# A delta-rule attention with a GELU block behind it: three narrow groups per slot in program order

## The chip, the cores and the metric

The kernel runs on one core of a Trainium2 chip. The metric is the device time of one execution in microseconds. Before the change it is 835.21 us, the median of three runs (832.89 to 837.22). The profiled execution spans 828.9 us; all times inside it count from its first instruction. Engines are TensorE (PE in the profile, its weight loads PEld), VectorE (DVE), ScalarE (ACT), GpSimd (POOL) and SyncE (SP, which issues most transfers).

## What is computed

```python
# attention: B, H, S, D = 4, 8, 768, 48
k_n = k / (norm(k, axis=-1) + 1e-6)
for t in range(S):
    y[:, :, t] = q[:, :, t] @ state                       # 48 x 48 state per batch and head
    v_old      = state^T @ k_n[:, :, t]
    state      = state + beta[:, :, t] * outer(k_n[:, :, t], v[:, :, t] - v_old)
# block: x is y as (3072, 384); w_in 384 x 2048, w_out 2048 x 384
h = x @ w_in
out = (h / (1 + exp(-1.702 * h))) @ w_out
```

The kernel does the recurrence in chunks of 128 positions: 6 chunks of 4 batches are 24 *units*. Inside a chunk it needs the scores of keys against keys (G), the inverse of a triangular 128 x 128 matrix per head (in four 32 x 32 diagonal blocks, which VectorE inverts for two units at a time, and a forward substitution over the four blocks on TensorE), and the masked scores of queries against keys (M). Two consecutive units together give 256 rows for the block behind.

## The kernel before

Work on TensorE is *wide* (the two big products, full 128 x 128 array, `ph` and `po`) or *narrow* (attention, on parts of the array). The program is a loop of slots, n from -1 to 24. In slot n three units are under way: A = n-1 (last substitution, outputs, new state), B_ = n (middle of its substitution), D_ = n+1 (scores, first block). Wide work waits in `queue`, a list of generators that yield the estimated cost of what they have just issued.

```python
class Engine:                       # an operation is pinned to the program's order if in_order[0]
    def __getattr__(self, name):
        op = getattr(self.engine, name)
        return pinned(op) if in_order[0] else op
vec, act, pe = Engine(nc.vector), Engine(nc.scalar), Engine(nc.tensor)
```

An operation that is not pinned is placed by the scheduler of the build, which may move it ahead of earlier ones that it takes to be waiting. Before, only slots up to 1 are pinned (`in_order[0] = n < HB`, HB = 2).

```python
def slot(n, share):                                        # GR = 6 groups
    A, B_, D_ = steps.pop(n - 1, None), steps.get(n), None
    P = prepare(n + B) if B <= n + B < len(units) else iter(())     # B = 4
    ...
    for group in range(GR):
        if group == 0:
            next(P, None)                                  # transposes of the keys
            D_ = steps.get(n + 1) or new_step(n + 1)
            next(D_.scored, None)                          # transposes of the queries
        elif group == 1:
            together([(B_, 1)], [(A, 2)])
            next(D_.scored, None)                          # first half of psQ
        elif group == 2:
            run(D_.scored)                                 # second half of psQ
        elif group == 3:
            together([(A, 3), (D_, 0)], [(B_, 1)])
            run(P)                                         # psG
        elif group == 4:
            if A: A.queries(); A.outputs()                 # psY
        else:
            together([(B_, 2)], [(D_, 0)])
            if A: A.state()                                # psS
        ...                                                # normalizing of later keys, from group 2
        if group == GR - 1 and n % HB == 1:
            m = n + 1 + HB
            if B <= m < len(units):
                inverting = invert(*units[m], HB)
        ahead_of(inverting, 5 if n % HB == 1 else 4)       # so many steps of the inversion
        ...                                                # conversion of weights, slots up to 3
        for cost in take(todo / (GR - group)):             # wide work
            todo -= cost
    if n % HB == 0:
        run(inverting)
    ...                                                    # loads; new wide work goes to the queue
```

The narrow operations, with the lines that the profile names:

```python
def together(solves, belows):
    psU = bank("psU") if solves else None
    psR = bank("psR") if belows else None
    for h in range(H):
        for X, blk in solves: X.solve(blk, h, psU)         # L552: 32 x 32 inverse times V
        for X, blk in belows: X.below(blk, h, psR)         # L541: G times the solved block
    for X, blk in solves: X.solved(blk, psU)               # L559: ScalarE copies psU to US
    for X, blk in belows: X.rest(blk, psR)                 # L548: VectorE, V -= psR

def scores(self):
    self.QS = wk.tile(...); self.M = wk.tile(...)          # three buffers each
    transposed(self.qp, self.QS[:, :, 0:128])              # L351 TensorE psT, L352 ScalarE
    if c > 0: act.activation(self.QS[:, :, S], St, ACT.Copy)   # L510: the state beside the queries
    yield
    for g in range(0, NP, 2):
        ps = [pool_.tile([128, 2, 128 + D], F32, ...) for _ in range(2)]
        ...                                                # L519: psQ, scores and k @ state
        for hh in range(2):
            if c > 0:
                vec.tensor_tensor(Vh, Vh, ps[hh][:, :, S], op=ALU.subtract)   # L527
            copy = act.copy if hh == 0 or self.n < 2 * B + HB else vec.tensor_copy
            copy(self.M[:, hs, :], ps[hh][:, :, 0:128])    # L529
        if g == 0: yield
    nc.gpsimd.affine_select(out=self.M, ...)               # L532: the mask

def queries(self):
    self.psY = [bank("psY", (128, 2, 128)) for _ in range(2)]
    ...                                                    # L568: queries times state
def outputs(self):
    ...                                                    # L568: M times US, into psY
    other = act.copy if self.c == 0 else vec.tensor_copy
    other(last[:, t], self.psY[1][:, 1, :])                # L609
    act.copy(self.xT[:, 0::2, t], self.psY[0])             # L610
    other(self.xT[:, 1, t], self.psY[1][:, 0, :])          # L611
    ...                                                    # small transfers complete xT
def state(self):
    psS = bank("psS", (128, NP, D))
    ...                                                    # L590: keys times US
    vec.tensor_tensor(St, psS, St, op=ALU.add)             # L595

def prepare(n):
    transposed(kn, kT, c == 0)                             # L351, L352
    yield 0.6
    ...                                                    # L366: psG, two banks
    act.activation(G[:, 0::2], ps[0], ACT.Copy)            # L370
    ...                                                    # L374 VectorE for later units
    ...                                                    # G goes to memory, its diagonal blocks come back as NT
```

`bank` takes one of four PSUM banks of the pool ps_seq; ps_big and ps_moe have two banks each. `invert` (L402 to L460) takes 25 steps for two units: a product with beta, 15 small rows (L426, L430), eight large products (L409, L410), and the end, after which the inverse goes through memory (Yd, XB) to where `solve` reads it. The weights come as 64-bit floats and are converted by VectorE (L181 to L193) in slots up to 3. The wide work:

```python
def hidden(xT, gT, t, cost):
    for f0 in range(0, FC, 2):                             # FC = 16
        ph = ps_moe.tile([128, 2, n], F32, ...)
        for u in range(2):
            ...                                            # L633: three matmuls (two instructions each)
            yield cost
        act.activation(gT[...], ph, ACT.Gelu_apprx_sigmoid)    # L638
def written(c, b0, gT):
    for i in range(HB):
        po = ps_moe.tile([128, DM], F32, ...)
        for f in range(FC):
            pe.matmul(po, lhsT=gT[...], rhs=w_out[:, f, :], ...)   # L648
            if f % 2 == 1 and f < FC - 1: yield 1.3
        vec.tensor_copy(o, po)                             # L655
        ...                                                # transfer out
        yield 1.3
```

Of the kernel before, what the change touches and what calls it, by code (L numbers as in the profile page):

```python
# [8 lines left out]
F32 = mybir.dt.float32  # L9
# [9 lines left out]
def kernel(  # L19
# [21 lines left out]
    B, H, S, D = q.shape  # L41
# [435 lines left out]
    def bank(name, shape=(128, H, D)):  # L477
        return ps_seq.tile(list(shape), F32, tag="seq", name=name)
# [3 lines left out]
    class Step:  # L482
# [19 lines left out]
        def scores(self):  # L502

            c, S = self.c, slice(128, 128 + D)
            self.QS = wk.tile([128, NP, 128 + D], F32, tag="QS", name="QS", bufs=3)
            self.M = wk.tile([128, H, 128], F32, tag="M", name="M", bufs=3)
            transposed(self.qp, self.QS[:, :, 0:128])
            if c > 0:
                St = ST[:, self.b, 0 : NP * D].rearrange("p (j d) -> p j d", j=NP)
                act.activation(self.QS[:, :, S], St, ACT.Copy)  # L510
            yield
            n = 128 + D if c > 0 else 128
            for g in range(0, NP, 2):
                pool_, tag = (ps_seq, "seq") if g else (ps_big, "big")
                ps = [pool_.tile([128, 2, 128 + D], F32, tag=tag, name="psQ") for _ in range(2)]
                for i in range(2):
                    for hh in range(2):
                        r = self.rows(hh)
                        pe.matmul(  # L519
                            ps[hh][:, i, 0:n], lhsT=self.kT[r, g + i, :],  # L520
                            rhs=self.QS[r, g + i, 0:n], start=True, stop=True,
                        )
                for hh in range(2):
                    hs = slice(2 * g + hh, 2 * g + 4, 2)
                    if c > 0:
                        Vh = self.V[:, hs, :]
# [3 lines that stand above are left out]
                if g == 0:  # L530
                    yield
            nc.gpsimd.affine_select(  # L532
                out=self.M, in_=self.M, compare_op=ALU.is_gt, fill=0.0, base=0,
                pattern=[[0, H], [1, 128]], channel_multiplier=-1,
            )
# [35 lines left out]
                )  # L571

        def queries(self):
            self.psY = [bank("psY", (128, 2, 128)) for _ in range(2)]
            if self.c > 0:

                self.turned(
                    (0, 5, 4, 1, 2, 7, 6, 3),
                    lambda h: ST[self.rows(h), self.b, h // 2 * D : h // 2 * D + DP],
                    lambda h: self.QS[self.rows(h), h // 2, 0:128],  # L580
                    True,
                )

        def state(self):
            if self.c == NC - 1:
                return
            psS = bank("psS", (128, NP, D))
            for h in range(H):
                p = h % 2 * DP
                pe.matmul(  # L590
                    psS[p : p + DP, h // 2, :], lhsT=self.kn[:, h, :], rhs=self.U[:, h, :],
                    start=True, stop=True,
                )
            St = ST[:, self.b, 0 : NP * D].rearrange("p (j d) -> p j d", j=NP)
            vec.tensor_tensor(St, psS, St, op=ALU.add)  # L595

        def outputs(self):
            self.turned(
                (0, 4, 1, 5, 2, 6, 3, 7),
                lambda h: self.US[:, h * D : h * D + DP], lambda h: self.M[:, h, :],  # L600
                self.c == 0,
            )
            t = slice(self.b % HB * C, (self.b % HB + 1) * C)
            first = self.c == 0 and self.b < HB
            if t.start == 0:
                lasts[0] = wk.tile([128, NTH], F32, tag="o", name="last")
            last = lasts[0]
            other = act.copy if self.c == 0 else vec.tensor_copy
            other(last[:, t], self.psY[1][:, 1, :])  # L609
            act.copy(self.xT[:, 0::2, t], self.psY[0])  # L610
            other(self.xT[:, 1, t], self.psY[1][:, 0, :])  # L611

            if first or t.start > 0:
                t = t if first else slice(0, NTH)
                for ct in range(2):
                    for j in range(KC):
                        nc.sync.dma_start(
                            out=self.xT[ct * DP + D : (ct + 1) * DP, j, t],
                            in_=last[ct * DP + j * XR : ct * DP + (j + 1) * XR, t],
                        )  # L620


    def hidden(xT, gT, t, cost):

        n = t.stop - t.start
        for f0 in range(0, FC, 2):
            if f0 // FQ == len(gT):
                gT.append(wk.tile([128, FQ, NTH], F32, tag="gT", name="gT", bufs=GB))
            ph = ps_moe.tile([128, 2, n], F32, tag="moe", name="ph")
            for u in range(2):  # L630
                f = f0 + u
                for j in range(KC):
                    pe.matmul(  # L633
                        ph[:, u], lhsT=w_in[:, j, f * 128 : (f + 1) * 128], rhs=xT[:, j, t],
                        start=(j == 0), stop=(j == KC - 1),
                    )
                yield cost
            act.activation(  # L638
                gT[f0 // FQ][:, f0 % FQ : f0 % FQ + 2, t], ph, ACT.Gelu_apprx_sigmoid
            )  # L640

    def written(c, b0, gT):

# [25 lines left out]
    def weights(n, dma=nc.gpsimd.dma_start):  # L669
        for _ in range(n):  # L670
            if staged:
                convert(staged.pop(staged.index(min(staged))))
            if dma is not None:
                ahead(2, dma)
            yield 0.0

    def take(cost):

        while cost > 0 and queue:
            more = next(queue[0], None)  # L680
            if more is None:
                queue.pop(0)
            else:
                cost -= more
                yield more

    def run(work):
        for _ in work:
            pass
# [13 lines left out]
    def new_step(n):  # L703
        if n >= len(units):
            return NoStep()
        h = n // HB
        if h not in xTs:
            xTs[h] = wk.tile([128, KC, NTH], F32, tag="xT", name="xT", bufs=3)
        steps[n] = Step(n, xTs[h])
        return steps[n]  # L710

    def together(solves, belows):

        solves = [(X, blk) for X, blk in solves if X]
        belows = [(X, blk) for X, blk in belows if X]
# [3 lines that stand above are left out]
            for X, blk in solves:  # L719
                X.solve(blk, h, psU)  # L720
            for X, blk in belows:
                X.below(blk, h, psR)
        for X, blk in solves:
            X.solved(blk, psU)
        for X, blk in belows:
            X.rest(blk, psR)

    def slot(n, share):
# [48 lines left out]
                warm(NB0)  # L777
        if n + 1 == len(WB) - 1:
            run(weights(n_parts))
        if n % HB == 0:  # L780
            run(inverting)
        if B <= n + B < len(units):
            load(n + B, ((QP, q),), sync if n < B else nc.sync.dma_start)
        if n > 0:
            m = n - 1 + len(KN)
            if m < len(units):
                load(m, ((KN, k),), sync if n < B else nc.gpsimd.dma_start)
            if n - 1 + B < len(units):
                load_values(n - 1 + B)
            h = (n - 1) // HB  # L790
            if h == 0:
                i = (n - 1) % HB
                queue.append(hidden(xTs[h], gT0, slice(i * C, (i + 1) * C), 0.67))
            if n % HB == 0:
                gT = gT0 if h == 0 else []
                if h > 0:
                    queue.append(hidden(xTs[h], gT, slice(0, NTH), 1.3))
                queue.append(written(*units[h * HB], gT))
                xTs.pop(h)

    queue = []
    sync = pinned(nc.sync.dma_start)
# [30 lines left out]
    normalize_first(B, len(KN) - B)  # L833
    run(weights(W1))
    for n in range(-1, len(units) + 1):
        in_order[0] = n < HB

        slot(n, 15.6 if n <= B else 18.8 if n <= B + HB else 20.8)
    run(take(1e9))


# [28 lines left out]
```

## Time and profile before

| what | value |
|---|---|
| time, median of three | 835.21 us |
| span of the profiled execution | 828.9 us |
| ScalarE busy | 214.2 us (26%) |
| wide matmuls ph, po: instructions, mean modelled duration | 1248, 375 ns; 768, 495 ns |
| VectorE's subtraction of psR (L548) | 87 times, 556 ns |
| ScalarE's copy of psU (L559) | 88 times, 470 ns |
| transfers Yd and XB (inverse out and back), median to landing | 2.2 us, 3.1 us |
| transfer of keys, issued by GpSimd, median to landing | 3.5 us |

The page of the profile has busy times by engine, forty slices of the span with the busy share in tenths, and the chain of work that ended last. The timeline lists instructions in order of time; matmuls of one kind that follow each other are merged, with their count. A 32-bit matmul of the program appears as two instructions. Ends of matmuls are modelled, so start-to-start distances are the safer measure.

### The profile page before, as it was taken

What the parts mean: (1) busy time and instruction counts of PE and PEld (TensorE: products, weight loads), DVE (VectorE), ACT (ScalarE), POOL (GpSimd) and SP (SyncE); (2) the same over time, 40 slices, a digit from 0 to 9 for tenths busy, and PEclk for the clock granted to TensorE, in tenths of its full rate; (3) what the DMA queues carried; (4) which work ended last, traced back from release to release, by engine and by line L of the source; (5) the groups of instructions that cost most, each with busy time, mean ns of one, the idle gap of its engine ahead of it and who ended that gap; (6) DMA issues with size and microseconds to landing.
All of it is one profiled execution on the core that took longest, in us unless ns stands there. A gap on an engine that the chain in (4) does not pass through costs nothing.

```text
span 828.9 us, 18791 instructions
## 1 busy us (share of the span) xinstructions
PE 776.7 (94%) x8100; PEld 571.2 (69%) x8100; DVE 492.7 (59%) x1095; ACT 214.2 (26%) x441; POOL 119.2 (14%) x138
## 2 busy tenths in 40 slices
PE   8438799879999999999999999999999999999998
PEld 7327688547767867767767767767768768677684
DVE  6998889688785494493593592692692871110000
ACT  2303543242322322312213222222223213111020
POOL 2103120232022202202202202211200000000000
PEclk9559889999999999999999999999999999999999
DMA  9996731732314213213223123123123020000000
GB/s 144 205 155 150 199 83 56 175 83 51 68 40 92 62 32 79 62 47 78 50 61 77 36 63 84 28 64 85 24 58 78 1 60 2 11 16 2 24 1 19
DMA packets 147315, 55.97 MB, mean 68 GB/s; under 512 B 114336, under 2 KB 143232, under 8 KB 147232
## 3 DMA queue, kind: packets, MB, share of 16 engines
q1 hardware_dynamic: 139488, 41.96, 25.3%
q0 software_dynamic: 2752, 10.62, 4.3%
q10 hardware_dynamic: 4992, 2.20, 1.0%
q8 instruction: 63, 1.03, 0.5%
q14 instruction: 20, 0.16, 0.1%
HBM read 33.13 MB, written 20.45 MB: 65 GB/s over the span
## 4 chain that ended last, share of the span: by engine, by line
PE 68%; DVE 16%; issue 7%; DMA 6%; POOL 3%; ACT 1%; SPq 0%; DVEq 0%; POOLq 0%
PE ph L633 26%; PE po L648 24%; PE psU L552 4%; PE psY L568 4%; DMA KN<-in_k_dram 3%; PE psG L366 3%; PE psQ L519 2%; DVE P L426 2%; DVE YB L430 2%; DVE P L104 2%; DMA w_out<-in_moe_w_out_dram 2%; POOL rn L312 2%; PE psR L541 1%; PE psT L351 1%; PE psS L590 1%
## 5 line engine op out<-in xcount | busy, mean ns | idle before, releaser
L633 PE MATMUL ph<-xT,w_in 128*128 128x256 f32 (+1 forms) x1248 | 276.3, 375 | 1.8 <-DMA xT<-last 1.6
L648 PE MATMUL po<-w_out,gT 128*128 128x384 f32 x768 | 267.9, 495 | 5.6 <-DVE w_out L193 5.6
L633 PEld LDWEIGHTS ph<-xT,w_in 128*128 128x128 f32 x1248 | 222.0, 195 | 40.2 <-issue 8.9
L648 PEld LDWEIGHTS po<-w_out,gT 128*128 128x128 f32 x768 | 140.4, 190 | 95.9 <-DVE w_out L193 7.7
L638 ACT ACTIVATE gT<-ph 128x512 f32<-128x512 f32 (+1 forms) x104 | 58.7, 564 | 188.0 <-PE ph L633 188.0
L548 DVE TENSOR_TENSOR V<-V,psR 32x384 f32<-32x384 f32 x87 | 48.4, 556 | 91.0 <-PE psR L541 89.3
L559 ACT COPY US<-psU 32x384 f32<-32x384 f32 x88 | 41.3, 470 | 129.8 <-PE psR L541 112.7
L552 PEld LDWEIGHTS psU<-V,XB 32*32 32x32 f32 x1408 | 51.7, 106 | 33.1 <-issue 17.2
L552 PE MATMUL psU<-V,XB 32*32 32x48 f32 x1408 | 62.9, 205 | 4.0 <-DVE V L527 2.7
L532 POOL TENSOR_SCALAR_AFFINE_SELECT M<-M 128x1024 f32<-128x1024 f32 x24 | 27.4, 1142 | 264.7 <-DVE M L529 193.2
L541 PE MATMUL psR<-US,G 32*32 32x48 f32 x2080 | 60.5, 204 | 0.1
L655 DVE COPY o<-po 128x384 f32<-128x384 f32 x24 | 13.1, 544 | 66.3 <-PE po L648 66.1
L541 PEld LDWEIGHTS psR<-US,G 32*32 32x32 f32 x2080 | 50.1, 105 | 1.4 <-issue 0.7
L426 DVE TENSOR_TENSOR P<-NT,YB 64x2 f32<-64x2 f32 (+4 forms) x135 | 46.9, 347 | 4.0
L430 DVE TENSOR_REDUCE YB<-P 64x2 f32<-64x2 f32 (+4 forms) x135 | 43.3, 321 | 4.4
L519 PE MATMUL psQ<-QS,kT 48*128 48x176 f32 (+1 forms) x384 | 43.3, 352 | 2.1 <-ACT QS L352 2.1
L527 DVE TENSOR_TENSOR V<-V,psQ 128x96 f32<-128x96 f32 x80 | 17.4, 249 | 42.5 <-PE psQ L519 41.9
L519 PEld LDWEIGHTS psQ<-QS,kT 48*128 48x128 f32 x384 | 31.3, 208 | 14.7 <-issue 5.0
L529 ACT COPY M<-psQ 128x256 f32<-128x256 f32 x68 | 23.8, 374 | 64.1 <-DVE V L527 59.3
L89 POOL DMA_DIRECT2D KN<-in_k_dram x14 | 13.4, 957 | 182.6 <-PE psS L590 171.5
L153 PE MATMUL ps_warm<-ident 128*128 128x256 bf16 x152 | 22.4, 314 | 16.0 <-DVE ps_warm L104 13.7
L609 DVE COPY last<-psY 128x128 f32<-128x128 f32 x20 | 5.8, 288 | 52.6 <-PE psY L568 52.4
(118 smaller groups left out, 786.2 us busy)
## 6 DMA issues: line engine op xcount, KB each, us to landing
Nd<-G SPq DMA_DIRECT2D x20, 512.0 KB, 3.2
w_out<-in_moe_w_out_dram POOLq DMA_DIRECT2D x14, 384.0 KB, 4.1
QP<-in_q_dram SPq DMA_DIRECT2D x24, 192.0 KB, 3.2
V<-in_v_dram SPq DMA_DIRECT2D x24, 192.0 KB, 2.8
out_dram<-o SPq DMA_DIRECT2D x24, 192.0 KB, 2.7
w_out<-in_moe_w_in_dram SPq DMA_DIRECT2D x6, 576.0 KB, 13.2
NT<-Nd SPq DMA_DIRECT2D x24, 128.0 KB, 2.5
Yd<-YS SPq DMA_DIRECT2D x24, 128.0 KB, 2.2
```

The source lines that it names most:

```text
L426: tt(P, diag(Nf, i * BS, [[0, i], [1, i]]), diag(Yf, 0, [[BS, i], [1, i]]), op=ALU.mult,)
L430: red(diag(Yf, i, [[BS, i]]), P, axis=AX.X, op=ALU.add, negate=True)
L519: pe.matmul(ps[hh][:, i, 0:n], lhsT=self.kT[r, g + i, :], rhs=self.QS[r, g + i, 0:n], start=True, stop=True,)
L532: nc.gpsimd.affine_select(out=self.M, in_=self.M, compare_op=ALU.is_gt, fill=0.0, base=0, pattern=[[0, H], [1, 128]], channel_multiplier=-1,)
L541: pe.matmul(psR[u, h, :], lhsT=self.G[r, h, u], rhs=self.U[r, h, :], start=True, stop=True,)
L548: vec.tensor_tensor(self.V[u], self.V[u], psR[u], op=ALU.subtract)
L552: pe.matmul(psU[r, h, :], lhsT=inverse[self.n][r, h, :], rhs=self.V[r, h, :], start=True, stop=True,)
L559: act.copy(self.U[r], psU[r])
L568: pe.matmul(self.psY[h % 2][p : p + DP, s, :], lhsT=lhsT(h), rhs=rhs(h), start=start and s == 0, stop=True, skip_group_check=True,)
L633: pe.matmul(ph[:, u], lhsT=w_in[:, j, f * 128 : (f + 1) * 128], rhs=xT[:, j, t], start=(j == 0), stop=(j == KC - 1),)
L638: act.activation(gT[f0 // FQ][:, f0 % FQ : f0 % FQ + 2, t], ph, ACT.Gelu_apprx_sigmoid)
L648: pe.matmul(po, lhsT=gT[f // FQ][:, f % FQ, i * C : (i + 1) * C], rhs=w_out[:, f, :], start=(f == 0), stop=(f == FC - 1),)
```

## The change

From slot 4 on (B = 4) `woven` takes the place of `slot`, and everything that goes through `vec`, `act` and `pe` is pinned again. A slot has three narrow groups in place of six, with wide work between them measured by a running debt. The idea is to leave the wide work less often, to spread the inversion's steps over both slots of a pair, and to fix an order in which every narrow operation's inputs were asked for at least one stretch of wide work earlier. Details:

- Both halves of psQ run in group 1. The queries' transposes for the next unit stand near the end of the slot before.
- Queries, outputs, state and the keys' scores psG all stand in group 3. psS moves into the free columns of the first psY bank, as the four banks of the pool are all taken there.
- Keys are prepared five units ahead instead of four; slot 4 makes up for this with one extra preparation.
- The inversion gets 9, 5, 3 steps in odd slots and 3, 3, 3 in even ones (8 each in slot 4).
- From unit 3 on, ScalarE copies all of psY.
- `hidden` hands over after its GELU, not between matmul and GELU.

The diff, with blank lines and an unchanged helper's surroundings cut:

```diff
             self.QS = wk.tile([128, NP, 128 + D], F32, tag="QS", name="QS", bufs=3)
-            self.M = wk.tile([128, H, 128], F32, tag="M", name="M", bufs=3)
             transposed(self.qp, self.QS[:, :, 0:128])
...
             yield
+            self.M = wk.tile([128, H, 128], F32, tag="M", name="M", bufs=3)
...
         def queries(self):
-            self.psY = [bank("psY", (128, 2, 128)) for _ in range(2)]
+            whole = [bank("psY", (128, 512)) for _ in range(2)]
+            self.psY = [w[:, 0:256].rearrange("p (s t) -> p s t", s=2) for w in whole]
+            self.psS = whole[0][:, 256 : 256 + NP * D].rearrange("p (j d) -> p j d", j=NP)
...
-        def state(self):
+        def state(self, psS=None):
...
-            psS = bank("psS", (128, NP, D))
+            psS = bank("psS", (128, NP, D)) if psS is None else psS
...
-            other = act.copy if self.c == 0 else vec.tensor_copy
+            other = act.copy if self.c == 0 or self.n >= B - 1 else vec.tensor_copy
...
-                yield cost
+                if u == 0:
+                    yield cost
             act.activation(
                 gT[f0 // FQ][:, f0 % FQ : f0 % FQ + 2, t], ph, ACT.Gelu_apprx_sigmoid
             )
+            yield cost
...
+        if n == B - 1:
+            next(new_step(n + 2).scored, None)
...
+    def spend(cost):
+        debt[0] += cost
+        for done in take(debt[0]):
+            debt[0] -= done
+
+    STEPS = (9, 5, 3, 3, 3, 3)
+
+    def woven(n, share):
+        nonlocal inverting
+        A, B_, D_ = steps.pop(n - 1, None), steps.get(n), steps.get(n + 1) or NoStep()
+        m, late = n + B + 1, n == B
+        K = normalize(m) if m < len(units) else iter(())
+        P = prepare(m) if m < len(units) else iter(())
+        Q = prepare(m - 1) if late else iter(())
+        if n % HB == 1 and n + 1 + HB < len(units):
+            inverting = invert(*units[n + 1 + HB], HB)
+        ahead = [8] * 3 if late else STEPS[:3] if n % HB == 1 else STEPS[3:]
+
+        next(K, None)
+        next(Q, None)
+        together([(B_, 1)], [(A, 2)])
+        run(D_.scored)
+        next(K, None)
+        ahead_of(inverting, ahead[0])
+        spend(share / 3)
+
+        together([(A, 3), (D_, 0)], [(B_, 1)])
+        run(Q)
+        next(K, None)
+        ahead_of(inverting, ahead[1])
+        spend(share / 6)
+        next(P, None)
+        spend(share / 6)
+
+        together([(B_, 2)], [(D_, 0)])
+        if A:
+            A.queries()
+            A.outputs()
+            A.state(A.psS)
+        run(P)
+        ahead_of(inverting, ahead[2])
+        if n % HB == 0:
+            run(inverting)
+        spend(share / 6)
+        next(new_step(n + 2).scored, None)
+        spend(share / 6)
+        follow(n)              # the loads and queue entries that ended slot() before
...
     for n in range(-1, len(units) + 1):
-        in_order[0] = n < HB
-        slot(n, 15.6 if n <= B else 18.8 if n <= B + HB else 20.8)
+        in_order[0] = n < HB or n >= B
+        step = slot if n < B else woven
+        step(n, 15.6 if n <= B else 18.8 if n <= B + HB else 20.8)
```

More of the change, by code (lines that the diff above doesn't have):

```diff
@@ L591, in state @@
                     psS[p : p + DP, h // 2, :], lhsT=self.kn[:, h, :], rhs=self.U[:, h, :],
-                    start=True, stop=True,
+                    start=True, stop=True, skip_group_check=True,
                 )
@@ L779, in slot, with follow @@
             run(weights(n_parts))
+        if n == B - 1:
+            next(new_step(n + 2).scored, None)
         if n % HB == 0:
             run(inverting)
+        follow(n)
+    def follow(n):
         if B <= n + B < len(units):
@@ L799, in slot @@
                 xTs.pop(h)
+    debt = [0.0]
+    def spend(cost):
[39 more added lines that the diff above has]
+        spend(share / 6)
+        follow(n)
     queue = []
```

## Prediction

> **What bounds the kernel now.** I read the page first: busy times, the slices of the span, the chain that ended last.
>
> ```profile
> PE 776.7 (94%) x8100; PEld 571.2 (69%) x8100; DVE 492.7 (59%) x1095; ACT 214.2 (26%) x441; POOL 119.2 (14%) x138
> PE   8438799879999999999999999999999999999998
> DVE  6998889688785494493593592692692871110000
> PE 68%; DVE 16%; issue 7%; DMA 6%; POOL 3%; ACT 1%; SPq 0%; DVEq 0%; POOLq 0%
> ```
>
> TensorE is busy in nine tenths or more of every slice from the eleventh on, about 207 us. The windows view is sharper: 1.8 us of TensorE idleness in the 393 us from 258 to 651, none from 651 to 784. So there a saving must come out of TensorE's own time; before about 220 us waits count. VectorE swings between 2 and 9 tenths: the inversion sits in every second slot. Next the timeline of TensorE in one slot (start us, duration us, operation, count, and in brackets idle time before it with its releaser).
>
> ```profile
> 481.98 0.23 PE L552 MATMUL psU<-V,XB 32*32 32x48 f32 x1 [0.51 <-DVE V L527]
> ...
> 506.73 0.87 PE L519 MATMUL psQ<-QS,kT 48*128 48x176 f32 x8
> 507.53 4.15 PE L633 MATMUL ph<-xT,w_in 128*128 128x256 f32 x18
> 511.61 0.23 PE L552 MATMUL psU<-V,XB 32*32 32x48 f32 x2
> ...
> 517.60 0.67 PE L568 MATMUL psY<-QS,ST 48*64 48x128 f32 x16
> 518.19 1.09 PE L568 MATMUL psY<-M,US 128*64 128x128 f32 x16
> 519.22 2.86 PE L633 MATMUL ph<-xT,w_in 128*128 128x256 f32 x12
> ...
> 526.55 0.60 PE L351 MATMUL psT<-ident,QP 128*128 128x128 f32 x4
> 526.99 2.76 PE L633 MATMUL ph<-xT,w_in 128*128 128x256 f32 x12
> 529.58 1.45 PE L648 MATMUL po<-w_out,gT 128*128 128x384 f32 x4
> ```
>
> Modelled ends overlap, so I take start-to-start distances. Wide work alone shows at the end of the chain:
>
> ```profile
> 784.17 20.72 PE ph L633 x96
> 804.89 20.66 PE po L648 x64
> ```
>
> That is 0.216 us per ph instruction and 0.323 per po. Eighteen ph should take 3.88 us, but from 507.53 to 511.61 they take 4.08, and twelve po between narrow work take 4.07 in place of 3.87: **one narrow stop inside wide work costs 0.20 to 0.21 us** beyond its matmuls. The stretch after the transposes, 526.99 to 529.58, takes 2.59 for a pure 2.59: full-array transposes cost no switch. A slot has five tiled stops (substitution with psQ; psQ; substitution with psG; psY; substitution with psS) and one stop of transposes: in the slot from 501.05 to 530.96 I count 8.2 us of narrow work, 20.65 of pure wide work and 1.05 of switches, together its 29.9 us. Other slots are up to 0.8 longer, because psU waits for VectorE's subtraction L527, queued behind inversion steps, as the first line shows.
>
> **What the Trainium skill says.** "TensorEngine Tiling (Array Packing)", section Key Properties: changing the tiling mode drains TensorE. The trace agrees: 0.21 us for a tiled stop, nothing for a 128x128 transpose. "PSUM — Partial Sum Buffer", section on bank collisions: no two engines may touch one bank and quadrant at once, so accesses must be guarded by bank, not by address. The trace agrees that this kernel is built so: ScalarE's copy M (columns 0 to 127 of psQ) waits for VectorE's subtraction (columns 128 to 175 of the same bank), though both only read:
>
> ```profile
> ACT M L529 <- DVE V L527: 59.3, 40, 5.0
> ```
>
> Same page, section "Engine vs sequencer instructions": VectorE's and ScalarE's queues are strict FIFO and matmuls run in program order. With everything pinned, a wait at the head holds all behind it, as in the bracket above.
>
> **The change part by part.**
>
> 1. *Fewer stops.* In a steady slot five tiled stops become three; the keys' and queries' transposes stand apart, but cost no switch. 2 x 0.21 = 0.42 us. The two psQ batches become one: from the last psQ start to the next operation is 0.24 us, the stride of its pairs about 0.17, so 0.07 to 0.09 more. Together **0.5 us a slot**, for slots 7 to 20: 14 x 0.5 = 7.0. Slots 21 to 24 have fewer stops already; there I count 5 stops saved in all and two psQ merged: 1.2. Sum **-8.2 us**.
>
> 2. *Inversion in small helpings.* From one keys' transpose to the next, slots last 29.91 to 30.72 us. Taking 29.9 as the undisturbed slot, the thirteen from 253.65 to 647.65 add up to **5.2 us** of excess, nearly all the subtraction behind inversion steps. With 9, 5, 3 and 3, 3, 3 steps a helping is 3.5 to 4.8 us of VectorE (small steps 0.3 to 1.2 us a pair, the large ones of L409 and L410 2 to 4 us), plus some 3 us for the first group's other work; 6.9 us of wide work and the group lie between it and the next. It fits. **-5.2 us**.
>
> 3. *The state behind the outputs, in psY's bank.* New: psS shares a bank with psY[0], so its matmuls wait for ScalarE to empty psY[0]; psG stands behind them and waits too. The outputs leave by ScalarE in the order last (psY[1]), xT (psY[0]), xT (psY[1]). Before, VectorE's copy `last` starts at 519.33, 0.11 us after psY's stretch. In its place ScalarE starts then, needs about 0.2 us more until the next copy can start (durations 0.27; back-to-back starts overlap by 0.1) and 0.37 for xT: done at 519.9, and a hand-over of about 0.1 (my estimate from such gaps). Instead of 519.22, psS starts at about 520.05: **+0.85 us a slot** of plain TensorE idleness. Slots 7 to 20: **+11.9 us**. ScalarE itself has room (26% busy).
>
> Slots 7 to 24 give -8.2 - 5.2 + 11.9 = **-1.5 us**: the gain goes into a new wait.
>
> 4. *The changeover, slots 4 to 6.* The transposes at 170.3 and 253.65 mark these slots: 83 us. In the kernel before, wide work floats: by 170.3 it has run 46 of the first 64 po instructions, both po tiles in turn as each piece of w_out is converted. Under the program's order slots up to 3 own only 16 of them; 30 x 0.323 = 9.7 us move into slot 4. And the first third of slot 4's wide work is pieces 8 to 15 of the first po tile, which needs the last w_out. VectorE finishes that late, and units 6 and 7's inverse later:
>
> ```profile
> 186.44 0.56 DVE L193 SCALAR_TENSOR_TENSOR w_out<-tmp,w_out 128x384 f32<-128x384 f32 x1
> 215.46 1.22 DVE L460 TENSOR_TENSOR YS<-YB,bI 64x1024 f32<-64x1024 f32 x1
> ```
>
> So TensorE stands in slot 4 until about 187, then has some 18 us of that slot left (with one extra preparation, 1.5), then slot 5's first group and 6.3 us of wide work: about 214 us. There unit 6's substitution needs its inverse. VectorE's work from 170.5 to it is 8.8 (conversions) + 5.6 (slot 4's own) + 23.4 (the inversion) = 37.8, so 208, and 5 to 6 us of transfers (2.2 and 3.1 by the DMA issues): the same 214. Then 19.3 us of slot 5 and 28.4 of slot 6 end at about 262 against 253.65: **+8 us**. If conversions run earlier, because fewer VectorE operations cut in, the loss may vanish, or the changeover gain 4, since the old slots 5 and 6 hold chopped-up narrow groups (31 and 32 us against some 28). I give two thirds to +8 and one third to -4: **+4**.
>
> Sum: 835.2 - 1.5 + 4 = 837.7. I shade this to **836 us**: details such as the extra preparation look tuned to a trace that I have not seen.
>
> **Rivals.** (a) *Switches and waits only*: if psS need not wait for ScalarE, or the wait is some 0.3 us, the steady part gains 9 to 13 us and the kernel ends at 822 to 830, at 818 with a smooth changeover. For it: the columns do not overlap. Against it: the M copies. (b) *VectorE becomes the bound in pinned order*: any helping that overruns its gap stops TensorE. For it: slot 4 has 8 steps a group with conversions still running. Against it: 59% busy, evenly spread. If it overran by 1 us per slot: 853. (c) *ScalarE delays the ph buffers*: a GELU behind copies that wait would stop TensorE, as ph has two buffers, one pair of blocks each (2.6 us). The GELU is now issued before each break, so I expect nothing. (d) *Transfers*: keys are loaded, normalized and transposed within one slot, 3.5 us of landing against some 8; hidden.
>
> **Range and chances.** 836 us, 820 to 850 eight times in ten. Faster by over 2% is below 818.5: rival (a) with a smooth changeover, 0.09. Slower by over 2% is above 851.9: (b), or psS waiting longer, 0.08. Within 2%: 0.83.
>
> **What would show it.** Step 1: three tiled stops per slot and psQ x16 in one piece. Step 2: no psU waiting for L527. Step 3: before each psS from slot 4 on, 0.7 to 0.9 us of TensorE idleness with ScalarE's xT as its releaser; if absent, I am wrong towards faster. Step 4: TensorE idle at about 176 to 187 before po, and slot 7's first group some 8 us later than 258.5; if it comes before 255, I have mis-sized the changeover. Long waits of TensorE on VectorE after 260 us would make the prediction wrong towards slower.

## The result and the profile after

The changed kernel takes **846.07 us** (median of four, 845.02 to 846.96) against 835.19 before: ratio 1.0143, 95% interval 1.0108 to 1.0178. It is slower by 10.9 us. Pinned operations all carry line 104, that of the helper, so they are told apart by tile. The page, with the same rows as before and the granted clock:

```profile
PE 766.7 (91%) x8100; PEld 574.2 (68%) x8100; DVE 499.2 (59%) x1055; ACT 221.0 (26%) x481; POOL 134.2 (16%) x138
PE   8439889477999999999999999999999999999998
DVE  6898999589776656566666666666656551100000
PEclk9659898679999999999999999999999999999999
PE 69%; DVE 19%; issue 7%; DMA 2%; ACT 2%; POOL 1%; DVEq 0%; POOLq 0%; ACTq 0%
```

VectorE is now even, 5 to 6 tenths in every slice of the steady part: the inversion was spread as intended. TensorE is busy for less time than before (766.7 against 776.7 us) in a longer span: it does the same 8100 matmuls with fewer overheads and stands more. Where it stands shows in the timeline of TensorE within one odd slot (some rows left out):

```profile
394.80 2.75 PE L104 MATMUL ph<-xT,w_in 128*128 128x256 f32 x12
398.82 1.56 PE L104 MATMUL ph<-xT,w_in 128*128 128x256 f32 x6 [1.27 <-DVE o L104]
...
409.05 0.67 PE L104 MATMUL psY<-QS,ST 48*64 48x128 f32 x16
409.64 1.09 PE L104 MATMUL psY<-M,US 128*64 128x128 f32 x16
411.42 0.67 PE L104 MATMUL psY<-US,KN 128*64 128x48 f32 x16 [0.68 <-ACT xT L104]
412.02 1.16 PE L104 MATMUL psG<-kT 48*128 48x128 f32 x16
```

The row `psY<-US,KN` is the state's psS, now in psY's bank. It waits for ScalarE, as predicted. The wait in the first pair of rows was not predicted: the second block of ph needs the bank from which VectorE has yet to copy po. VectorE's own timeline has the reason; the copy comes last after a helping of inversion:

```profile
397.57 0.29 DVE L104 TENSOR_TENSOR P<-NT,YB 64x128 f32<-64x128 f32 x1
398.20 0.56 DVE L104 COPY o<-po 128x384 f32<-128x384 f32 x1
```

From first group to first group, slots 7 to 18 before last 29.91 us at best and up to 31.3. After, they alternate: 31.1 to 31.6 with this wait, 29.97 without. TensorE's two waits in the steady part, 266 to 800 us (us in total, times, longest):

```profile
PE psY L104 <- ACT xT L104: 9.3, 14, 0.7
PE ph L104 <- DVE o L104: 6.1, 7, 1.3
```

Its longest waits between 150 and 266 us, the changeover:

```profile
PE psT L104 <- POOL KN L316: 12.5, 2, 8.4
PE po L652 <- DVE w_out L193: 3.5, 1, 3.5
PE po L104 <- DVE w_out L193: 2.3, 2, 1.4
```

The clock granted to TensorE was lower there too. From 155 to 178 us, first in the kernel before, then in the changed one (columns: stretch, its length, busy us and instructions of TensorE, its loads, VectorE, ScalarE, GpSimd, then clock, DMA share, GB/s):

```profile
155.00:178.00 23.00, 18.01 (x256) 10.95 (x257) 16.83 (x42) 8.69 (x19) 9.60 (x11) 0.93 0.50 128
155.00:178.00 23.00, 12.99 (x181) 10.58 (x182) 15.30 (x35) 6.36 (x13) 7.11 (x9) 0.50 0.59 134
```

Slot 7's first group stands at 266.46, before at 258.50. From there to the end the profiles have 577.5 and 570.4 us, but the changed kernel has 5.1 us more wide work left at that point, and one psG less (1.1 us). On equal work the steady part is thus 3 us worse (7.1 - 5.1 + 1.1), and the changeover 12 of the 15 us between the two profiles. By the medians it is some 8 of 10.9: the profiled execution before, 828.9 us, is a quick one, and the conversion phase varies by several us between executions: in two kernels further down that are unchanged up to slot 7, slot 7's first group stands at 262.1 and 263.6.

### The profile page after: what moved, and what is told of

Same layout as the page of the kernel before. It is cut to its first block, busy times and chain, and to the rows that moved or that the text cites. A ratio compares the mean times of both kernels' runs of the same rounds, so it can differ in the third digit from the quotient of the medians.

```text
span 843.9 us, 18733 instructions
## 1 busy us (share of the span) xinstructions
PE 766.7 (91%) x8100; PEld 574.2 (68%) x8100; DVE 499.2 (59%) x1055; ACT 221.0 (26%) x481; POOL 134.2 (16%) x138
## 3 DMA queue, kind: packets, MB, share of 16 engines
q8 instruction: 63, 1.03, 0.5%
## 4 chain that ended last, share of the span: by engine, by line
PE 69%; DVE 19%; issue 7%; DMA 2%; ACT 2%; POOL 1%; DVEq 0%; POOLq 0%; ACTq 0%
PE ph L104 25%; PE po L104 24%; PE psY L104 5%; PE psU L104 4%; DVE P L104 3%; DVE YB L104 2%; PE psQ L104 2%; DVE NT L104 2%; PE psG L104 2%; PE psT L104 2%; PE psR L104 2%; PE ps_warm L153 2%; DMA w_out<-in_moe_w_out_dram 2%; DVE V L104 1%; DVE w_in L104 1%
## 5 line engine op out<-in xcount | busy, mean ns | idle before, releaser
L104 PE MATMUL ph<-xT,w_in 128*128 128x256 f32 x1056 | 242.8, 383 | 6.2 <-DVE o L104 6.1
L104 PEld LDWEIGHTS ph<-xT,w_in 128*128 128x128 f32 x1056 | 196.1, 190 | 40.1 <-DVE o L104 9.2
L104 DVE TENSOR_TENSOR V<-V,psR 64x384 f32<-64x384 f32 (+1 forms) x88 | 48.9, 556 | 165.2 <-PE psR L104 164.2
L104 DVE TENSOR_TENSOR P<-NT,YB 64x18 f32<-64x18 f32 (+25 forms) x190 | 92.3, 486 | 5.3 <-DVE YB L104 0.3
L104 ACT ACTIVATE gT<-ph 128x512 f32<-128x512 f32 x88 | 52.5, 597 | 155.5 <-PE ph L104 155.4
L104 DVE TENSOR_REDUCE YB<-P 64x6 f32<-64x18 f32 (+25 forms) x190 | 80.7, 425 | 6.2
L104 PEld LDWEIGHTS psU<-V,XB 32*32 32x32 f32 x1408 | 50.4, 106 | 30.8 <-issue 25.9
L532 POOL TENSOR_SCALAR_AFFINE_SELECT M<-M 128x1024 f32<-128x1024 f32 x24 | 31.1, 1294 | 234.4 <-DVE M L104 163.7
L312 POOL TENSOR_TENSOR rn<-ssq,half 128x8 f32<-128x8 f32 x17 | 39.1, 2298 | 21.6 <-DVE ssq L104 20.2
L104 DVE TENSOR_TENSOR P<-NT 64x256 f32<-64x256 f32 (+7 forms) x40 | 34.0, 849 | 0.3
L104 DVE TENSOR_REDUCE NT<-P 64x64 f32<-64x1024 f32 (+7 forms) x40 | 32.5, 814 | 1.3
L153 PEld LDWEIGHTS <-ident 128*128 128x128 bf16 x152 | 17.4, 116 | 20.7 <-issue 13.7
L635 PE MATMUL ph<-xT,w_in 128*128 128x128 f32 x192 | 29.0, 312 | 2.4 <-DMA xT<-last 2.4
```

The costliest lines, as they stand in the source:

```text
L104: return lambda *a, **kw: tc.keep_in_program_order(op(*a, **kw))
L153: pe.matmul(ps, lhsT=ones[:, 0:128], rhs=ones, start=True, stop=True)
L312: nc.gpsimd.tensor_tensor(rn, ssq, half, op=ALU.pow)
L532: nc.gpsimd.affine_select(out=self.M, in_=self.M, compare_op=ALU.is_gt, fill=0.0, base=0, pattern=[[0, H], [1, 128]], channel_multiplier=-1,)
L635: pe.matmul(ph[:, u], lhsT=w_in[:, j, f * 128 : (f + 1) * 128], rhs=xT[:, j, t], start=(j == 0), stop=(j == KC - 1),)
```

## The experiments

Ratios are to the kernel before, timed on the same chip. Its median was 834.0 us beside the first four kernels, 834.8 beside the next, 836.7 beside the three from psS and po on, 832.7 beside the last, so kernels of different groups are best compared by their ratios.

**Scores ahead of the state.**

```diff
             A.outputs()
-            A.state(A.psS)
         run(P)
+        if A:
+            A.state(A.psS)
```

> Edit: in group 3 the keys' scores psG come before the state's matmuls psS; nothing is added or removed. Theory (psS waits about 0.73 us for ScalarE to empty psY[0], and psG waits behind it): psG's 1.09 us covers the wait, so 15 of the 17 slots with a state lose it, 12 of them in the steady part: 8 to 11 us less, about 836 us, and no idle time of TensorE before psS in those slots. Rival (the idle time is a hand-over that any order pays, or it is not on TensorE's path): 846 us, within 2 us.

Measured: 835.28 us, ratio 1.002 (0.9992 to 1.0047). Of the waits of psS after 266 us two are left, in the slots that prepare no keys:

```profile
PE psY L104 <- ACT xT L104: 1.3, 2, 0.7
```

In the changed kernel there were 14 in the same stretch. An undisturbed slot shrinks from 29.97 to 29.26 us. The wait was on TensorE's path, and other work covers it.

**po copied by ScalarE.** `-            vec.tensor_copy(o, po)` becomes `+            act.copy(o, po)`.

> Edit: ScalarE instead of VectorE copies po out. Theory (in every odd slot the second ph block waits 1.05 to 1.5 us for that copy, which stands behind nine inversion steps in VectorE's order): the seven waits of ph vanish, 8.6 us less, about 837 us; intervals between first groups become 29.9 to 30.0 us throughout. Rival (another operation takes its place, such as a copy of po held up behind ScalarE's own queue): 843 to 846 us.

Measured: 836.85 us, ratio 1.0037 (1.002 to 1.0055). The waits of ph are gone, nearly all intervals are 29.97 to 30.06 us. ScalarE's queue took the copy without a new kind of wait; the longest wait of psS grew from 0.7 to 1.0 us.

**A later start.** Every `B` that marks the first new slot becomes 8.

```diff
-        m, late = n + B + 1, n == B
+        m, late = n + B + 1, n == 8
-        in_order[0] = n < HB or n >= B
-        step = slot if n < B else woven
+        in_order[0] = n < HB or n >= 8
+        step = slot if n < 8 else woven
```

> Edit: the new kind of slot and the pinning begin at slot 8 instead of 4, with the extra preparation moved there. Theory (12 us of the loss come from the changeover meeting the conversion of weights and the late inverse of units 6 and 7): the changeover costs 0 to 4 us, so 834 to 838 us. Rival (the changeover costs the same wherever it is, since it squeezes one extra preparation and 24 inversion steps into one slot): 843 to 847 us.

Measured: 841.13 us, ratio 1.0075 (1.0045 to 1.0106), between the two. My expectation left out the 3 us by which the steady part alone is worse; with them the first theory says 837 to 841. So a changeover at slot 8 is cheaper, though not free: TensorE still waits 3.6 us there for the extra keys. Every second slot still lasts 31.2 to 31.5 us; the wait of ph is put down to ScalarE's GELU in this profile (4.5 us, 6 times). In the next kernel, where po's copy moves as well, it is gone.

**The three together.**

> Edit: the three edits of the other kernels together. Theory: from 835.2 take the switches (about 8 to 10 us for slots 8 to 24) and the waits for VectorE (5.2), add the two psS waits left (1.5) and 0 to 4 us of changeover: 820 to 826 us, faster than the kernel before by 1.1 to 1.8%. Rival (the mended waits let another one come out, VectorE at 59% being close behind): 830 us or more.

Measured: 825.12 us, ratio 0.9884 (0.9839 to 0.9929): within the sum, at its upper end.

**A bank of its own for psS.** `-            A.state(A.psS)` becomes `+            A.state()`, in the same place.

> Edit on the changed kernel: psS gets a bank of its own again, in the same place of the order (behind the outputs, ahead of psG). Theory (the wait comes from the shared bank, not from the order): psS then waits for psU's bank only, which ScalarE empties while psY runs, so all 17 waits of about 0.73 us vanish: 9 to 12 us less, about 835 us. Rival (four banks are too few for group 3, so the wait moves to another narrow operation): 842 us or more, with idle time before psS, psY or psU.

Measured: 832.1 us, ratio 0.9976 (0.9956 to 0.9996). The timeline of TensorE:

```profile
310.68 0.67 PE L104 MATMUL psY<-QS,ST 48*64 48x128 f32 x16
311.28 1.09 PE L104 MATMUL psY<-M,US 128*64 128x128 f32 x16
312.20 0.62 PE L104 MATMUL psS<-US,KN 128*64 128x48 f32 x16
312.75 1.16 PE L104 MATMUL psG<-kT 48*128 48x128 f32 x16
```

From psY to psG it is 2.07 us, in the changed kernel 2.97 (409.05 to 412.02). From the second psY to psS it is 0.92 us (311.28 to 312.20), there 1.78. So the shared bank made the wait, and four banks suffice: the pool's other banks are emptied in time. Start to start the shared bank cost 0.86 us a slot, more than the idle time of 0.73 that the profile shows between modelled ends; 17 slots make 14.6. That is why the kernel gains 14 us where I expected 9 to 12.

**Nothing pinned.** `in_order[0] = n < HB or n >= B` becomes `in_order[0] = n < HB`.

> Edit on the changed kernel: the new slots keep their order of issue, but nothing from slot 2 on is pinned. Theory (the changeover loses 12 us because wide work can no longer float into the waits of slots 3 to 5): most of that comes back, 8 to 12 us less, 834 to 838 us, while the waits of psS stay. Rival (the changeover loses because of its extra preparation and 24 inversion steps, pinned or not): 843 us or more.

Measured: 843.0 us, ratio 1.0076 (1.0049 to 1.0102). The theory fell. Wide work does float: by 170 us 40 instructions of po have run, against 16 when pinned. But slot 7's first group starts at 267.42, no earlier than 266.46. From 190 to 221 TensorE is busy for all 31.0 us, but at a granted clock of 0.80; when pinned it is busy for 26.2 us at 0.94. Busy time times clock is nearly the same, 24.8 and 24.6. And VectorE finishes the inverse of units 6 and 7 later, at 227.2 (its last product) where the changed kernel has 212.5. What the kernel gained (ratio 1.0076 against 1.0143) lies in the steady slots: against my expectation the waits of psS are gone there, those of ph too (together 15.4 us), and the scheduler's order brings a wait of its own, 10.0 us in six places after 266:

```profile
PE po L652 <- ACT gT L641: 10.0, 6, 3.3
```

**Both steady waits taken away, start at slot 4** (scores ahead of the state, po by ScalarE), and **the same, pinned only from slot 6**.

> Edit on the changed kernel: psG ahead of psS, and po copied by ScalarE, begin at slot 4 as in the change. Theory (the two waits are separate): their gains of about 9 to 10 us each add up, 826 to 829 us. Rival (they overlap, or VectorE comes out as the next bound): 832 us or more.

> Edit on the kernel before this one (psG ahead of psS, po by ScalarE): slots 4 and 5 have the new shape but are not pinned; pinning begins at slot 6. Theory (what costs in the changeover is that wide work can't float into the waits for keys and weights): 6 to 12 us less than that kernel, 816 to 822 us. Rival (the shape of slot 4, with its extra preparation, is what costs): the same as that kernel within 2 us.

Measured: 826.6 us, ratio 0.9904 (0.9875 to 0.9933), so the two gains add up; and 827.98 us, ratio 0.9915 (0.989 to 0.994), no gain from floating. In the second kernel VectorE's last conversion starts at 196.2 and the inverse's last product at 226.1 (in the first at 185.1 and 212.2), and from 170 to 200 TensorE, though busy for 29.3 of 30 us, ran at a granted clock of 0.55. VectorE was busy for only 19.0 us there, against 25.3 in the first kernel (first row: first kernel, second and third: second kernel; columns as above):

```profile
170.00:200.00 30.00, 23.73 (x236) 14.73 (x236) 25.29 (x65) 8.35 (x17) 5.01 (x5) 0.79 0.19 49
170.00:200.00 30.00, 29.34 (x234) 18.60 (x234) 18.97 (x49) 9.94 (x22) 5.94 (x6) 0.55 0.17 45
226.10 1.22 DVE L460 TENSOR_TENSOR YS<-YB,bI 64x1024 f32<-64x1024 f32 x1
```

**Own bank and po by ScalarE; then two edits of the changeover on top of it.**

> Edit on the changed kernel: psS in a bank of its own, and po copied by ScalarE. Theory (psS's wait and the ph block's wait are separate): the gain of the own bank (14 us) and 8 to 9 us add up, 822 to 826 us. Rival (they overlap): 830 us or more.

> Edit on the kernel before this one: in slot 4 half of the wide work comes ahead of the keys' transposes, and the first pair's two po tiles advance together, so that they need only the pieces of w_out converted by then. Theory A (the changeover loses because TensorE stands at the keys' transposes, 8 us at the start of slot 4): 5 to 8 us less than that kernel, 815 to 819 us. Theory B (the changeover ends when the inverse of unit 6 has landed, about 218 us, whatever TensorE did before): less than 2 us less, the idle time moves in front of unit 6's first substitution.

> Edit on the kernel before this one: in slot 5 two thirds of the wide work, not one, lie ahead of the group that needs unit 6's inverse. Theory B (that inverse is the gate, and what counts is how much wide work is done ahead of it): 4 to 7 us less than the kernel before this one. Theory A: the same within 2 us.

```diff
# wide first (on own bank and copy)
+        if late: spend(share / 2)         # ahead of the extra keys' transposes
         next(Q, None)
-        spend(share / 3)
+        spend(0.0 if late else share / 3)
...
-        spend(share / 6)                  # the one after next(P, None)
+        spend(0.0 if late else share / 6)
# the first pair: both po tiles piece by piece, for f: for i: pe.matmul(po[i], ...)
# wide before the inverse (on wide first): in slot 5
+        spend(share * 2 / 3)              # in place of share / 3; the rest of the slot has half
```

Measured: 822.86 us, ratio 0.9845 (0.9799 to 0.9891), with no wait of TensorE at all from 266 to 800; 821.48 us, ratio 0.983 (0.9788 to 0.9872); 821.16 us, ratio 0.9845 (0.9774 to 0.9915). The last two can't be told from the first: with four runs each, even some 5 us either way can't be excluded. With the wide work first, the waits for the keys shrink from 11.3 to 3.8 us, and another takes their place. All waits of TensorE from 150 to 266 us add up to 18.4, 19.7 and 21.3 us in the three kernels. The new one:

```profile
PE psU L104 <- DVE V L104: 11.3, 1, 11.3
```

So taking the wait for the keys away was not enough, and the inverse was not the next gate either. TensorE now stands for V, which VectorE subtracts only after the last conversion (second kernel):

```profile
183.19 0.56 DVE L193 SCALAR_TENSOR_TENSOR w_out<-tmp,w_out 128x384 f32<-128x384 f32 x1
183.78 0.56 DVE L104 TENSOR_TENSOR V<-V,psR 32x384 f32<-32x384 f32 x1
```

Early in this wait, until 175.12, VectorE itself stood for 3.25 us for a transfer of w_out.

**The switch alone, in the kernel before.** From slot 7 on (`if n > 6`) group 1 runs all of psQ.

> Edit on the kernel before the change: from slot 7 on both halves of psQ run in one piece, 8 + 8 instructions in place of 8, wide work, 8. TensorE's order is otherwise the same. Theory (a narrow stop inside wide work costs 0.21 us, and the joined psQ 0.07 to 0.09 less): 15 or 16 slots (D_ from unit 8 to 23) by 0.29 us are 4 to 5 us less, ratio 0.994 to 0.995. Rival (the switch is only how modelled ends look, or a wait for VectorE takes its place): ratio within 0.002 of 1.

Measured: 832.57 us, ratio 0.9994 (0.997 to 1.0018): the rival. But the trace has both effects. Slots without a wait shrink from 29.91 to 29.52 us. The slots between grow, from 30.8 to 31.1 on average, by waits that were not there (ph for transfers of `last`, 3.4 us in three places; ph for VectorE, 2.7 us in two):

```profile
503.43 1.87 PE L633 MATMUL ph<-xT,w_in 128*128 128x256 f32 x6 [1.37 <-DMA xT<-last]
506.02 1.46 PE L519 MATMUL psQ<-QS,kT 48*128 48x176 f32 x16
```

Here `last` comes from VectorE, still behind inversion steps, and its transfers end after ph wants them. The switch costs what the trace says; TensorE just arrives sooner at the next wait.

## Why the prediction was right or wrong

The time lies in the range, 10 us above its centre. By steps:

- **Fewer stops: right, too small.** With both steady waits gone (psS in its own bank, po by ScalarE), an undisturbed slot takes 29.16 us with the same amount of wide work (20.7 us) as the 29.91 before: 0.75 us are saved where I had 0.5. psQ in one piece takes 1.39 to 1.40 us against twice 0.80: that term was mis-sized, 0.20 and not 0.07 to 0.09. The second psY and psS, now joined, take 1.47 against 1.03 + 0.60, which I did not count. Fourteen slots give 10.5 in place of 7.0.
- **Inversion in small helpings: this step failed.** The waits of psU (5.2 us) are gone, but "It fits" looked only at the next group. po's copy stands behind the helping too, and seven slots lose 1.1 to 1.6 us each, 8.6 in all. Rival (b) had the mechanism, a helping of VectorE that stops TensorE, and put it down as unlikely. Rival (c) had the right buffers, two banks for ph and po, and the wrong engine: "so I expect nothing" thought of the GELU alone.
- **psS in psY's bank: right.** 0.86 us a slot start to start (29.97 against 29.11 with a bank of its own) where I had 0.85, so 12.0 for slots 7 to 20 against 11.9. That it agrees so closely is partly luck: 519.9 and the hand-over of 0.1 give 520.0, not 520.05. Both ways of undoing it, order and bank, bear out the mechanism.
- The steady sum, with the forecast 1.2 of slots 21 to 24 kept: -10.5 - 1.2 - 5.2 + 12.0 + 8.6 = +3.7, where the profiles have 3 and I had -1.5.
- **The changeover: the delay right, its places partly wrong.** I had 8 us, then weighed it down to 4. Slot 7's first group came 7.96 us late, and short of wide work besides. But TensorE stood less before po (2.3 us of pinned waiting) than at the keys' transposes (12.5), and the clock granted from 122 to 190 us was 0.77, where the kernel before had 0.95. And executions vary by some 5 us here, so the agreement with 8 us is partly luck.
- **The shading was wrong.** The unshaded sum with +8 was 841.7; I moved away from it because the details looked tuned. The plain sum was the better guess.

What stays open is what binds the changeover. Floating wide work (pinning from slot 6), moving it ahead, and giving more of it ahead of the inverse each shrank the wait aimed at and left the median within 2 us. One candidate is VectorE, with conversions and one inversion to finish in slots 3 to 5. It fits the wait for V. It does not fit the kernel pinned from slot 6: there VectorE was busy for 19.0 us from 170 to 200, and TensorE for 29.3 at a clock of 0.55. So the granted clock is a second candidate. No kernel took work from VectorE there, and none held the clock, so both are argued and not shown.

## What to carry to other kernels

When an order is fixed, ask of every operation of an in-order engine who waits for it, also of the rare ones: a copy once in two slots, about every 61 us, behind a helping of background work cost TensorE more (8.6 us) than the spreading had saved (5.2). In this kernel free columns of a bank still being emptied were not free; give the second user its own bank or other work to stand behind. And a saving on the engine that bounds the time is only kept if the next input arrives sooner too; where it doesn't, the time is handed back, as in the last experiment. With its two steady waits removed (psS in a bank of its own, po by ScalarE), the new slot is faster than both kernels: 822.86 us, ratio 0.9845.

## What was not expected of the hardware

TensorE's granted clock was 0.55 over 30 us in which it counted as busy for 29.3, in the kernel pinned from slot 6; four instructions of psQ then took 1.47 us start to start, where eight took 0.80 in the kernel before. So a TensorE that counts as busy can be a slow one. Waits of 1.2 and 2.1 us with short pieces of work between them came before it; that they brought the clock down is not shown.
